# More buffers, a re-ordered convolution loop and a lighter final stage in a kernel that trains a gated FFN beside an S4 convolution

## The chip, the cores and the metric

One core of one Trainium2 chip. The metric is device time in microseconds (us) of one execution; lower is better. The kernel before took 1850.78 us (median of 6, 1848.61 to 1853.17).

## The reference, cut to what matters

A layer norm feeds two branches, a state-space convolution with a skip and a gated FFN; the sum with the input is the output. The kernel computes the output and all gradients for an incoming gradient of the same shape.

```python
def _A_ref(u, ...):                          # L, D, N = 2048, 576, 128
    K = einsum("dn,dnl,dn->dl", C, exp(dt*A*l), dt*B).real
    y = irfft(rfft(u, 2L) * rfft(K, 2L))[:L]
    return y + u * Dskip
def _B_ref(x, W_gate, W_up, W_down):         # F = 4608
    return (relu(x @ W_gate) * (x @ W_up)) @ W_down
x = A_u
xn = layernorm(x)
out = x + _A_ref(xn, ...) + _B_ref(xn, ...)
# ... cut: jax.vjp of this function; 13 outputs
```

## The kernel before

Everything runs on one core. The FFN goes over 12 chunks of F and keeps TensorE busy. The S4 branch is a generator that is advanced beside it: the Fourier transforms are matmuls, the spectra are multiplied on VectorE. Every generator yields an estimate of its own length, and the S4 branch is advanced as long as its sum stays below 0.9 of the FFN's. The last convolution stage is `p3` of the second half; after it the last FFN chunk also carries the final stage, in which the convolution's result, the FFN and the layer norm's gradient are added up. When the program is built, a scheduler then fixes the order of each engine's instructions.

Names of tiles (buffers) that come up often: osx is an output tile of the FFN, fA a result of the first transform, s_ug and s_k are spectra of the signals and of the convolution's kernel, pr_t, pr_w and pr_z belong to their product, fC is a result of the last transform ("unmix"; "mix" makes the spectra). hN, dgT, duT, hT and upm are the FFN's. To evict is to copy a result out of PSUM, where matmuls leave it.

```python
PACE = 0.9
# ... cut
        self.op = pool("ffn_o", 3)                       # osx: two output tiles' halves
# ... cut: an output tile of the FFN, stored with accumulation
            nc.gpsimd.dma_start(g.acc_dram[:, t, :, :], o[:], accum_op=ALU.add)
# ... cut: product of two spectra, conj for the gradient
        t = wpool.tile([P, 2, DH], BF16, name="pr_t")
        w = wpool.tile([P, 2, DH], BF16, name="pr_w")
        v.tensor_tensor(t[:], A, B, op=ALU.mult)
        v.tensor_tensor(w[:, 0, :], A[:, 0, :], B[:, 1, :], op=ALU.mult)
        v.tensor_tensor(w[:, 1, :], A[:, 1, :], B[:, 0, :], op=ALU.mult)
        Z = pool.tile([P, 2, DH], BF16, name="pr_z")
        # two sums on 64 partitions from t into Z[0:64], two from w into Z[64:P]
# ... cut: last stage of the convolution, h = 0..16
                old, Z = Z, None
                if h < ST:
                    # ... mix the kernel's spectrum into sk
                    Z = self.product(zp, pp, sg[:, 0], sk[:], False), self.product(zp, pp, sg[:, 1], sk[:], True)
                    yield 0.7
                if old is not None:
                    for i in range(2):
                        Ct = fp.tile([P, 2, 1, DH], BF16, name="fC2")
                        yield from self.unmix(Ct[:, :, 0, :], old[i])
                        nc.sync.dma_start(self.mix_in(self.C[2][hf], h - 1)[:, :, i:i + 1, :], Ct[:])
                        yield 0.5
# ... cut: final stage; load() runs two row tiles ahead
        nc.vector.tensor_tensor(base[:], xg[:], self.dsk[:].unsqueeze(1).to_broadcast([P, 2, D]), op=ALU.mult)
# ... cut: take() of each half of each output
        self.g.nc.vector.tensor_tensor(dst, base[:, i, cols], ps, op=ALU.add)
```

## Time and profile before

| | before |
|---|---|
| median, us | 1850.78 |
| profiled execution: span, us | 1848.1 |
| TensorE busy, us | 1740.9 |
| half-clock stretches of TensorE, us | 34 in seven pieces |

Two more views are needed later. First the last three parts of the run as windows (start and end, length, then busy us of TensorE, its weight loads, VectorE, ScalarE and GpSimd with their numbers of instructions, TensorE's clock, DMA share and GB/s). They are the last convolution stage, the rest of the chunk, and the last chunk with the final stage:

```profile
1536.00:1616.00 80.00, 68.13 (x446) 37.23 (x444) 73.95 (x247) 58.22 (x159) 6.91 (x8) 0.96 0.89 241
1616.00:1698.00 82.00, 79.16 (x658) 54.65 (x656) 19.67 (x42) 26.90 (x61) 6.90 (x8) 0.98 0.67 185
1698.00:1808.00 110.00, 98.14 (x765) 68.81 (x763) 90.91 (x200) 47.83 (x93) 0.00 (x0) 1.00 0.69 217
```

VectorE has three different lives: over nine tenths busy, a quarter busy, and over eight tenths busy. TensorE is short of work, or of released work, in the first and the third: 11.9 of 80 and 11.9 of 110 us idle.

Second, one product on VectorE (start, length, engine, line, operation, tiles, count):

```profile
1607.62 0.46 DVE L665 TENSOR_TENSOR pr_t<-s_ug,s_k 128x576 bf16<-128x576 bf16 x1
1608.00 0.30 DVE L666 TENSOR_TENSOR pr_w<-s_ug,s_k 128x288 bf16<-128x288 bf16 x1
1608.22 0.30 DVE L667 TENSOR_TENSOR pr_w<-s_ug,s_k 128x288 bf16<-128x288 bf16 x1
1608.43 0.61 DVE L671 TENSOR_TENSOR pr_z<-pr_t 64x288 bf16<-64x288 bf16 x2
1609.08 0.64 DVE L674 TENSOR_TENSOR pr_z<-pr_w 64x288 bf16<-64x288 bf16 x2
```

The records of the multiplications overlap: the next starts 0.22 us after one that lasts 0.30.

### The profile page before, as it was taken

What the parts mean: (1) busy time and instruction counts of PE and PEld (TensorE: products, weight loads), DVE (VectorE), ACT (ScalarE), POOL (GpSimd) and SP (SyncE); (2) the same over time, 40 slices, a digit from 0 to 9 for tenths busy, and PEclk for the clock granted to TensorE, in tenths of its full rate; (3) what the DMA queues carried; (4) which work ended last, traced back from release to release, by engine and by line L of the source; (5) the groups of instructions that cost most, each with busy time, mean ns of one, the idle gap of its engine ahead of it and who ended that gap; (6) DMA issues with size and microseconds to landing.
All of it is one profiled execution on the core that took longest, in us unless ns stands there. A gap on an engine that the chain in (4) does not pass through costs nothing. (4 is left out here: it accounts for less than half of the span.)

```text
span 1848.1 us, 41883 instructions
## 1 busy us (share of the span) xinstructions
PE 1740.9 (94%) x16257; PEld 1180.4 (64%) x16257; DVE 1378.3 (75%) x3223; ACT 1173.1 (63%) x2647; POOL 205.9 (11%) x246
## 2 busy tenths in 40 slices
PE   7989989999999999999999999998999998899988
PEld 5655547667666666766666766766666765476666
DVE  7565975786897787787887889889878757923882
ACT  5865855686587488477477567657747737732442
POOL 0200002111012012002102101202201100010000
PEclk9989989999999999999999999999999999999999
DMA  8798989668567566766676756855755779885763
GB/s 292 264 325 290 338 235 269 194 174 237 168 129 205 185 178 169 210 187 149 189 202 136 234 157 153 235 163 121 188 166 115 163 240 268 220 213 159 247 214 100
DMA packets 236411, 373.26 MB, mean 202 GB/s; under 512 B 49202, under 2 KB 153140, under 8 KB 234676
## 3 DMA queue, kind: packets, MB, share of 16 engines
q1 hardware_dynamic: 210244, 304.08, 50.6%
q0 software_dynamic: 24384, 51.92, 18.1%
q10 hardware_dynamic: 1584, 14.60, 2.3%
q8 instruction: 127, 2.08, 0.5%
q14 instruction: 72, 0.59, 0.1%
HBM read 233.08 MB, written 137.43 MB: 200 GB/s over the span
## 5 line engine op out<-in xcount | busy, mean ns | idle before, releaser
L244 PE MATMUL ps_mm<-xT,wd 128*128 128x512 bf16 x1440 | 357.0, 379 | 0.7 <-ACT xT L153 0.7
L244 PEld LDWEIGHTS <-wd 128*128 128x128 bf16 x2145 | 194.9, 98 | 179.6 <-issue 8.5
L68 ACT CAST osx<-ps_mm 128x288 bf16<-128x288 f32 x684 | 261.9, 423 | 72.9 <-PE ps_mm L300 59.8
L313 POOL DMA_DIRECT2D acc_dram<-osx x160 | 139.3, 875 | 1037.8 <-ACT osx L68 581.5
L300 PE MATMUL ps_mm<-wf,dgT 128*128 128x288 bf16 x1152 | 209.0, 288 | 18.0 <-ACT osx L68 12.8
L354 PEld LDWEIGHTS <-rows 128*128 128x128 bf16 x1536 | 145.9, 98 | 98.2 <-issue 4.2
L300 PE MATMUL ps_mm<-wf,duT 128*128 128x288 bf16 x1152 | 207.6, 288 | 0.0
L300 PE MATMUL ps_mm<-wf,hT 128*128 128x288 bf16 x1152 | 185.4, 287 | 8.0 <-ACT osx L68 2.4
L929 DVE TENSOR_TENSOR pr<-X,ps_s 128x256 f32<-128x256 f32 x288 | 120.4, 418 | 85.1 <-PE ps_s L925 82.7
L244 PE MATMUL ps_mm<-gT,wd 128*128 128x512 bf16 x705 | 178.6, 379 | 0.4 <-ACT obw L68 0.4
L254 DVE SCALAR_TENSOR_TENSOR upm<-rg,ps_mm 128x512 bf16<-128x512 bf16 x144 | 98.4, 684 | 99.8 <-PE ps_mm L244 82.9
L68 ACT COPY YT<-ps_s 128x1024 bf16<-128x1024 bf16 x144 | 146.9, 1020 | 22.7 <-PE ps_s L911 20.1
L338 PE MATMUL ps_mm<-rows,hN 128*128 128x144 bf16 x2304 | 159.9, 229 | 0.0
L338 PEld LDWEIGHTS <-hN 128*128 128x128 bf16 x2304 | 150.7, 99 | 7.8 <-issue 5.2
L300 PEld LDWEIGHTS <-dgT 128*128 128x128 bf16 x1152 | 109.5, 98 | 55.3 <-issue 27.5
L354 PE MATMUL ps_mm<-duN,rows 128*128 128x384 bf16 x768 | 138.6, 326 | 0.5 <-DVE upm L254 0.5
L354 PE MATMUL ps_mm<-dgN,rows 128*128 128x384 bf16 x768 | 136.6, 326 | 1.3 <-DMA rows<-xs_dram 1.3
L300 PEld LDWEIGHTS <-hT 128*128 128x128 bf16 x1152 | 107.1, 98 | 41.3 <-issue 12.0
L300 PEld LDWEIGHTS <-duT 128*128 128x128 bf16 x1152 | 113.0, 98 | 29.8 <-issue 0.2
L68 ACT CAST obw<-ps_mm 128x384 bf16<-128x384 f32 x105 | 50.0, 477 | 127.0 <-PE ps_mm L354 90.8
L68 ACT CAST dhb<-ps_mm 128x512 bf16<-128x512 f32 x141 | 83.8, 595 | 63.7 <-PE ps_mm L244 62.1
L930 DVE TENSOR_REDUCE Sm<-pr 128x8 f32<-128x256 f32 x288 | 120.0, 417 | 3.6
(215 smaller groups left out, 3148.5 us busy)
## 6 DMA issues: line engine op xcount, KB each, us to landing
acc_dram<-osx POOLq DMA_DIRECT2D x176, 288.0 KB, 4.6
gT<-in_gT_dram SPq DMA_DIRECT2D x48, 640.0 KB, 6.4
xT<-xT_dram SPq DMA_DIRECT2D x44, 640.0 KB, 5.8
rows<-in_gq_dram SPq DMA_DIRECT2D x48, 576.0 KB, 4.4
rows<-xs_dram SPq DMA_DIRECT2D x48, 512.0 KB, 5.3
wd<-in_Wd_dram SPq DMA_DIRECT2D x36, 480.0 KB, 5.6
wf<-in_Wf_dram ACTq DMA_DIRECT2D x11, 1296.0 KB, 9.1
ex_dram<-exs SPq DMA_DIRECT2D x18, 640.0 KB, 5.3
```

The source lines that it names most:

```text
L68: self.nc.scalar.copy(out, in_)
L244: nc.tensor.matmul(ps[:], lhsT=w[:, k, fs], rhs=rhs[:, k, :], start=(k == 0), stop=(k == NK - 1))
L254: nc.vector.scalar_tensor_tensor(upm[:], rg[:], 0.0, ps_u[:], op0=ALU.is_gt, op1=ALU.mult)
L300: nc.tensor.matmul(ps[:, :DH], lhsT=lt, rhs=rh, start=(i == 0), stop=(i == len(mms) - 1))
L313: nc.gpsimd.dma_start(g.acc_dram[:, t, :, :], o[:], accum_op=ALU.add)
L338: nc.tensor.matmul(ps[:, ft * 144:(ft + 1) * 144], lhsT=self.hN[:, st, ft * P:(ft + 1) * P], rhs=gq[:, st, :], start=(st == 0), stop=(st = ...
L354: nc.tensor.matmul(ps[:, :Fc], lhsT=xs[:, st, 0:P], rhs=src[:, st, :], start=(st == 0), stop=(st == ST - 1))
L929: nc.vector.tensor_tensor(pr[:], X[:, dx:dx + DG, r0:r0 + 2].rearrange("p d r a -> p d (r a)").unsqueeze(2).to_broadcast(sh), psg[:, 0:DG ...
L930: nc.vector.tensor_reduce(out=Sm[:, vi, s0 + dd:s0 + dd + DG, :], in_=pr[:], op=ALU.add, axis=AX.X)
```

## The change

Its intent is to take the waits away that TensorE's list shows: a fourth osx buffer; the exponentials of the first stage in halves with 8 buffers and a pool of their own for the first transform's outputs (fA); deeper pools and an interleaved order in the last convolution stage; a product with one scratch buffer, which pays for these buffers; and a final stage in which ScalarE evicts and sums rows, while the skip becomes part of the convolution kernel's first tap.

```diff
-        self.op = pool("ffn_o", 3)
+        self.op = pool("ffn_o", 4)
 ... (exponentials: par_ex 3 -> 8 buffers, tiles of SX instead of 2*SX, twice as many steps)
-            yield from self.fwd1(hf, 2, load, ap, n, gap)
+            yield from self.fwd1(hf, 2, load, ap, self.pool(c, f"p1_o{hf}", 2 * n - 2 * (n < 4), "right"), n, gap)
 ... (the same in p3; p1_f, p3_f: 2 -> n buffers, p3_z: 3 -> n; n is 4 in the first and the last stage, else 2)
         v.tensor_tensor(t[:], A, B, op=ALU.mult)
-        v.tensor_tensor(w[:, 0, :], A[:, 0, :], B[:, 1, :], op=ALU.mult)
-        v.tensor_tensor(w[:, 1, :], A[:, 1, :], B[:, 0, :], op=ALU.mult)
 ... (the two sums from t)
+        v.tensor_tensor(t[:, 0, :], A[:, 0, :], B[:, 1, :], op=ALU.mult)
+        v.tensor_tensor(t[:, 1, :], A[:, 1, :], B[:, 0, :], op=ALU.mult)
 ... (the two other sums, now from t)
                     yield from self.mix(sk[:], b[:, :, 0, :])
-                    Z = self.product(zp, pp, sg[:, 0], sk[:], False), self.product(zp, pp, sg[:, 1], sk[:], True)
-                    yield 0.7
-                if old is not None:
-                    for i in range(2):
-                        ... (unmix of old[i], store)
-                        yield 0.5
+                    yield 0.35
+                for i in range(2):
+                    if h > 0:
+                        ... (unmix of Z[i], store)
+                    if h < ST:
+                        Z[i] = self.product(zp, pp, sg[:, i], sk[:], i == 1)
+                    yield 0.7
 ... (skip: Kst[0:1, 0, :] += dsk, once per group of 32 channels)
-        nc.vector.tensor_tensor(base[:], xg[:], self.dsk[:].unsqueeze(1).to_broadcast([P, 2, D]), op=ALU.mult)
-        self.g.nc.vector.tensor_tensor(dst, base[:, i, cols], ps, op=ALU.add)
+        if i == 0:
+            self.g.bal.copy(self.o[:, 0, cols], ps, DH)
+        else:
+            self.g.nc.scalar.activation(self.dx[:, cols], ps, ACT.Copy, accum_out=self.m[:, hf:hf + 1])
```

More of the change, by code (lines that the diff above doesn't have):

```diff
@@ L294, in outdx @@
                     mms = [(Ts[ft][1], self.wf[:, 1, ft, hs]) for ft in range(FTC)] + [(Ts[ft][2], self.wf[:, 2, ft, hs]) for ft in range(FTC)]
-                mms = [(lt[:, js], rh) for lt, rh in mms]
+                mms = [(lt[:, js], rh, slice(0, DH)) for lt, rh in mms]
                 if last is not None:
-                    mms = last.terms(t, which, hf) + mms
+                    mms = [(a, b, slice(0, DH)) for a, b in last.terms(t, which, hf)] + mms
                 ps = g.psum_mm.tile([P, 512], F32, name="ps_mm")
-                for i, (lt, rh) in enumerate(mms):
-                    nc.tensor.matmul(ps[:, :DH], lhsT=lt, rhs=rh, start=(i == 0), stop=(i == len(mms) - 1))
+                for i, (lt, rh, cs) in enumerate(mms):
+                    nc.tensor.matmul(ps[:, cs], lhsT=lt, rhs=rh, start=(i == 0), stop=(i == len(mms) - 1))
                 if last is None:
@@ L303, in outdx @@
                 else:
-                    last.take(t, which, hs, ps[:, :DH])
+                    last.take(t, which, hf, hs, ps[:, :DH])
                 next(src, None)
@@ L566, in params @@
             pool = self.pool(c, "par_raw", 1)
-            exp_ = self.pool(c, "par_ex", 3)
+            exp_ = self.pool(c, "par_ex", 8)
             raw = pool.tile([P, 6, D], BF16, name="raw")
@@ L581, in ex_step @@
             def ex_step(i):
-                shp = [P, 2 * SX, NE]
+                shp = [P, SX, NE]
                 ex = exp_.tile(shp, F32, name="exs")
-                v.tensor_tensor(ex[:], pw[:, 0, i * SX:(i + 2) * SX].unsqueeze(2).to_broadcast(shp), self.ev[:].unsqueeze(1).to_broadcast(shp), op=ALU.mult)
+                v.tensor_tensor(ex[:], pw[:, 0, i * SX:(i + 1) * SX].unsqueeze(2).to_broadcast(shp), self.ev[:].unsqueeze(1).to_broadcast(shp), op=ALU.mult)
                 nc.scalar.activation(ex[:], ex[:], ACT.Exp)
-                nc.sync.dma_start(self.ex_dram[:, i:i + 2], ex[:].rearrange("p (i d) e -> p i d e", d=SX))
-                bal.add(d=1.4, a=1.2)
-            for i in range(0, 8, 2):
+                nc.sync.dma_start(self.ex_dram[:, i], ex[:])
+                bal.add(d=0.75, a=0.65)
+            for i in range(0, 8):
                 ex_step(i)
-                yield 2.0
+                yield 1.0
             p1 = pool.tile([P, D], F32, name="p1")
@@ L601, in params @@
                 yield 2.0
-            for i in range(8, D // SX, 2):
+            for i in range(8, D // SX):
                 ex_step(i)
-                yield 2.0
+                yield 1.0
     def dft(self, pool, dram):
@@ L612, in dft, with fwd1 @@
         return load
-    def fwd1(self, hf, ns, load, ap, n, gap):
+    def fwd1(self, hf, ns, load, ap, op, n, gap):
         g, nc = self.g, self.g.nc
@@ L622, in fwd1 @@
                     yield gap
-            A = ap.tile([P, 2, ns, DH], BF16, name=f"fA{ns}")
+            A = op.tile([P, 2, ns, DH], BF16, name=f"fA{ns}")
             for ri in range(2):
@@ L662, in product @@
         t = wpool.tile([P, 2, DH], BF16, name="pr_t")
-        w = wpool.tile([P, 2, DH], BF16, name="pr_w")
+        Z = pool.tile([P, 2, DH], BF16, name="pr_z")
         v = nc.vector
         v.tensor_tensor(t[:], A, B, op=ALU.mult)
-        v.tensor_tensor(w[:, 0, :], A[:, 0, :], B[:, 1, :], op=ALU.mult)
-        v.tensor_tensor(w[:, 1, :], A[:, 1, :], B[:, 0, :], op=ALU.mult)
-        Z = pool.tile([P, 2, DH], BF16, name="pr_z")
         for i in range(2):
@@ L671, in product @@
             v.tensor_tensor(Z[0:64, i, :], t[r, 0, :], t[r, 1, :], op=ALU.add if conj else ALU.subtract)
+        v.tensor_tensor(t[:, 0, :], A[:, 0, :], B[:, 1, :], op=ALU.mult)
+        v.tensor_tensor(t[:, 1, :], A[:, 1, :], B[:, 0, :], op=ALU.mult)
         for i in range(2):
             r = slice(i * 64, (i + 1) * 64)
-            v.tensor_tensor(Z[64:P, i, :], w[r, 1, :], w[r, 0, :], op=ALU.subtract if conj else ALU.add)
+            v.tensor_tensor(Z[64:P, i, :], t[r, 1, :], t[r, 0, :], op=ALU.subtract if conj else ALU.add)
         g.bal.add(d=1.6)
@@ L698, in load @@
                 return lambda i, n2: t[:, i, n2 % 2, :]
-            yield from self.fwd1(hf, 2, load, ap, n, gap)
+            yield from self.fwd1(hf, 2, load, ap, self.pool(c, f"p1_o{hf}", 2 * n - 2 * (n < 4), "right"), n, gap)
         with ExitStack() as c:
             bp = self.pool(c, f"p1_b{hf}", n, "right")
-            fp = self.pool(c, f"p1_f{hf}", 2, "right")
+            fp = self.pool(c, f"p1_f{hf}", n, "right")
             pp = self.pool(c, f"p1_p{hf}", 1, "right")
@@ L764, in load @@
                 return lambda i, n2: kk[:, :, n2 % 4, :]
-            yield from self.fwd1(hf, 1, load, ap, n, gap)
+            yield from self.fwd1(hf, 1, load, ap, self.pool(c, f"p3_o{hf}", 2 * n - 2 * (n < 4), "right"), n, gap)
         with ExitStack() as c:
             bp = self.pool(c, f"p3_b{hf}", n, "right")
-            fp = self.pool(c, f"p3_f{hf}", 2, "right")
-            zp = self.pool(c, f"p3_z{hf}", 3, "right")
+            fp = self.pool(c, f"p3_f{hf}", n, "right")
+            zp = self.pool(c, f"p3_z{hf}", n, "right")
             pp = self.pool(c, f"p3_p{hf}", 1, "right")
@@ L778, in p3 @@
             bs = Ahead(load_b, ST, n)
-            Z = None
+            Z = [None, None]
             for h in range(ST + 1):
-                old, Z = Z, None
                 if h < ST:
@@ L787, in p3 @@
                     yield from self.mix(sk[:], b[:, :, 0, :])
-                    Z = self.product(zp, pp, sg[:, 0], sk[:], False), self.product(zp, pp, sg[:, 1], sk[:], True)
-                    yield 0.7
-                if old is not None:
-                    for i in range(2):
-                        Ct = fp.tile([P, 2, 1, DH], BF16, name="fC2")
-                        yield from self.unmix(Ct[:, :, 0, :], old[i])
-                        nc.sync.dma_start(self.mix_in(self.C[2][hf], h - 1)[:, :, i:i + 1, :], Ct[:])
-                        yield 0.5
+                    yield 0.35
+                for i in range(2):
+                    if h > 0:
+                        Ct = fp.tile([P, 2, 1, DH], BF16, name="fC2")
+                        yield from self.unmix(Ct[:, :, 0, :], Z[i])
+                        nc.sync.dma_start(self.mix_in(self.C[2][hf], h - 1)[:, :, i:i + 1, :], Ct[:])
+                    if h < ST:
+                        Z[i] = self.product(zp, pp, sg[:, i], sk[:], i == 1)
+                    yield 0.7
     def p2_pools(self, c):
@@ L809, in p2 @@
         lv, parp, dkp, exp_, xp, xop, uvp, yop, ytp, gp = pools
+        self.kdp = parp
         pend, turned = [], []
@@ L903, in turn @@
         if dd + DG == SC:
+            h0 = hf * DH + gi * SC
+            dsk = self.kdp.tile([1, SC], BF16, name="dsk")
+            nc.sync.dma_start(dsk[:], self.Dskip[h0:h0 + SC].rearrange("(o d) -> o d", o=1))
+            nc.vector.tensor_tensor(Kst[0:1, 0, :], Kst[0:1, 0, :], dsk[:], op=ALU.add)
             nc.sync.dma_start(self.k_dram[hf][:, :, gi], Kst[:].rearrange("p (q a) d -> p q a d", q=4))
@@ L1040, in load @@
             pool = lambda name, bufs: self.ctx.enter_context(g.tc.tile_pool(name=name, bufs=bufs, reuse_waits="tile"))
-            self.dsk = pool("fin1", 1).tile([P, D], BF16, name="dsk")
-            nc.sync.dma_start(self.dsk[:], self.Dskip.rearrange("(o d) -> o d", o=1).to_broadcast([P, D]))
+            one = pool("fin1", 1)
+            self.nr = one.tile([P, ST], F32, name="nr")
+            nc.vector.tensor_scalar(self.nr[:], g.rinv[:], -1.0 / D, None, op0=ALU.mult)
             self.pool = pool("fin3", 3)
@@ L1055, in load @@
         nc.sync.dma_start(acc[:], g.acc_dram[:, t])
-        base = self.pool.tile([P, 2, D], F32, name="f_base")
-        nc.vector.tensor_tensor(base[:], xg[:], self.dsk[:].unsqueeze(1).to_broadcast([P, 2, D]), op=ALU.mult)
-        g.bal.add(d=1.2)
-        return S3, Ct, xt, xg, acc, base
+        return S3, Ct, xt, xg, acc
     def begin(self, t):
@@ L1065, in begin, with skip @@
         self.o = self.pool.tile([P, 2, D], BF16, name="f_o")
+        self.dx = self.pool.tile([P, D], F32, name="f_dx")
+        self.m = self.pool.tile([P, 5], F32, name="f_m")
+    def skip(self, hf):
+        h0 = hf * DH
+        for k in range(NK):
+            c0, c1 = max(k * P, h0), min((k + 1) * P, h0 + DH)
+            if c0 < c1:
+                yield k, slice(c0 - k * P, c1 - k * P), slice(c0 - h0, c1 - h0)
     def terms(self, t, i, hf):
-        S3, Ct, xt, xg, acc, base = self.parts[t]
+        S3, Ct, xt, xg, acc = self.parts[t]
         cols = slice(hf * DH, (hf + 1) * DH)
@@ L1071, in terms, with take @@
         return mms + [(self.g.ident_bf[:], r) for r in ([xt[:, cols]] if i == 0 else []) + [acc[:, i, cols]]]
-    def take(self, t, i, cols, ps):
-        base = self.parts[t][5]
-        dst = self.o[:, 0, cols] if i == 0 else base[:, 1, cols]
-        self.g.nc.vector.tensor_tensor(dst, base[:, i, cols], ps, op=ALU.add)
-        self.g.bal.add(d=0.37)
+    def take(self, t, i, hf, cols, ps):
+        if i == 0:
+            self.g.bal.copy(self.o[:, 0, cols], ps, DH)
+        else:
+            self.g.nc.scalar.activation(self.dx[:, cols], ps, ACT.Copy, accum_out=self.m[:, hf:hf + 1])
+            self.g.bal.add(a=0.4)
     def end(self, t):
         g, nc = self.g, self.g.nc
-        S3, Ct, xt, xg, acc, base = self.parts[t]
-        o = self.o
-        inv_d = 1.0 / D
-        xn, gt, dx = xg[:, 0, :], xg[:, 1, :], base[:, 1, :]
+        S3, Ct, xt, xg, acc = self.parts[t]
+        o, m, dx = self.o, self.m, self.dx[:]
+        xn, gt = xg[:, 0, :], xg[:, 1, :]
         nc.sync.dma_start(g.out0_v[:, t, :], o[:, 0, :])
-        m = self.pool.tile([P, 4], F32, name="f_m")
-        nc.scalar.activation(acc[:, 1, :], dx, ACT.Copy, accum_out=m[:, 0:1])
-        nc.vector.scalar_tensor_tensor(acc[:, 0, :], dx, 1.0, xn, op0=ALU.mult, op1=ALU.mult, accum_out=m[:, 1:2])
-        nc.vector.tensor_scalar(m[:, 2:3], m[:, 1:2], -inv_d, None, op0=ALU.mult)
-        nc.vector.tensor_scalar(m[:, 3:4], m[:, 0:1], -inv_d, g.rinv[:, t:t + 1], op0=ALU.mult, op1=ALU.mult)
-        nc.vector.scalar_tensor_tensor(dx, xn, m[:, 2:3], dx, op0=ALU.mult, op1=ALU.add)
-        nc.scalar.activation(dx, dx, ACT.Identity, scale=g.rinv[:, t:t + 1], bias=m[:, 3:4])
+        nc.vector.scalar_tensor_tensor(acc[:, 0, :], dx, 1.0, xn, op0=ALU.mult, op1=ALU.mult, accum_out=m[:, 2:3])
+        nc.vector.tensor_scalar(m[:, 3:4], m[:, 2:3], -1.0 / D, None, op0=ALU.mult)
+        nc.vector.tensor_scalar(m[:, 4:5], m[:, 0:1], m[:, 1:2], self.nr[:, t:t + 1], op0=ALU.add, op1=ALU.mult)
+        nc.vector.scalar_tensor_tensor(dx, xn, m[:, 3:4], dx, op0=ALU.mult, op1=ALU.add)
+        nc.scalar.activation(dx, dx, ACT.Identity, scale=g.rinv[:, t:t + 1], bias=m[:, 4:5])
         nc.vector.tensor_tensor(o[:, 1, :], dx, gt, op=ALU.add)
         nc.sync.dma_start(g.out1_v[:, t, :], o[:, 1, :])
-        g.bal.add(d=2.5, a=1.1)
+        g.bal.add(d=2.2, a=0.6)
 @with_exitstack
@@ L1195, in lay_out @@
     o["gq"] = gr.reshape(P, ST, 4, 144).transpose(2, 0, 1, 3)
+    dsk = zeros(NK, P, P)
+    for d, v in enumerate(inputs["A_Dskip"]):
+        dsk[d // P, d % P, d % P] = v
+    o["dsk"] = dsk.transpose(1, 0, 2)
     g, u, dn = inputs["B_W_gate"], inputs["B_W_up"], inputs["B_W_down"]
```

## The prediction

> **What bounds the kernel now.** I read the page first: engine shares, then the slices.
>
> ```profile
> span 1848.1 us, 41883 instructions
> ...
> PE 1740.9 (94%) x16257; PEld 1180.4 (64%) x16257; DVE 1378.3 (75%) x3223; ACT 1173.1 (63%) x2647; POOL 205.9 (11%) x246
> ...
> PE   7989989999999999999999999998999998899988
> ...
> PEclk9989989999999999999999999999999999999999
> DMA  8798989668567566766676756855755779885763
> ```
>
> TensorE bounds the whole run: it is idle for 1848.1 - 1740.9 = 107 us. The change gives it no work and takes none: both instruction orders hold the same matmuls, in another order. So every gain must come out of these 107 us, or out of time in which the clock is low. The slices show where that is: the first seventh, and the last quarter of the span. The middle is at 9 throughout.
>
> Next, TensorE's own list of waits, longest first:
>
> ```profile
> PE ps_mm L300 <- ACT osx L68: 15.2, 24, 2.2
> ...
> PE ps_s L654 <- ACT fC L68: 8.5, 8, 1.7
> PE pt L273 <- DVE dgT L262: 7.9, 7, 2.8
> PE ps_s L627 <- ACT fA L68: 7.7, 9, 3.2
> PE ps_s L684 <- DMA bC<-C_dk: 5.6, 1, 5.6
> PE ps_mm L300 <- DVE f_o L1076: 3.8, 4, 1.2
> ```
>
> Columns: total us, times, longest. The names are those of tiles whose pools the change deepens (osx, fC, fA) and of the final stage it rewrites (f_o; most of dgT, below). Only bC is not touched. That is some 43 us of the 107; many others are gaps too short to be listed.
>
> Third, windows around the longest stalls, for the granted clock (PEclk), and one window of the last convolution stage:
>
> ```profile
> 135.20:142.00 6.80, 5.84 (x45) 5.37 (x45) 2.64 (x4) 4.43 (x8) 0.00 (x0) 0.50 0.95 320
> 1647.30:1650.70 3.40, 3.40 (x32) 3.40 (x30) 0.00 (x0) 0.03 (x1) 0.86 (x1) 0.50 0.84 280
> ...
> 1590.00:1600.00 10.00, 8.22 (x57) 4.32 (x56) 9.57 (x33) 7.50 (x21) 0.86 (x1) 1.00 0.82 201
> ```
>
> Columns after the length: busy PE, PEld, DVE, ACT, POOL, clock, DMA share, GB/s. A stall of about 3 us is followed by 3.4 or 6.8 us at half clock. There are seven such stretches (at 108, 135, 244, 268, 1555, 1582 and 1647 us), 34 us together, which cost up to 17 us. In the last row VectorE is the full engine, 9.57 of 10 us, not TensorE.
>
> Last, the timeline at two stalls:
>
> ```profile
> 1645.49 0.82 DVE L62 CAST osx<-ps_mm 128x288 bf16<-128x288 f32 x2 [4.04 <-DMA acc_dram<-osx]
> 1646.00 0.53 PE L300 MATMUL ps_mm<-wf,dgT 128*128 128x288 bf16 x3 [2.84 <-DVE osx L62]
> ```
>
> An eviction has no free osx buffer until the accumulating store has landed; TensorE waits behind it.
>
> ```profile
> 1759.19 1.36 DVE L1057 TENSOR_TENSOR f_base<-f_xg,dsk 128x1152 f32<-128x1152 bf16 x1 [2.31 <-DMA f_xg<-in_grad_out_dram]
> 1760.47 0.42 DVE L262 TENSOR_TENSOR dgT<-dhb,upm 128x512 bf16<-128x512 bf16 x1
> ...
> 1760.95 0.40 PE L273 MATMUL pt<-ident_bf,dgT 128*128 128x128 bf16 x4 [2.81 <-DVE dgT L262]
> ```
>
> In the final stage the skip product stands at the head of VectorE's queue, waits for a load that nobody needs yet, and holds the FFN's dgT behind it.
>
> **What the Trainium skill says.** "TensorE: Matmul & The Clock Gate", Part 1 (the HAM clock gate): after an idle window of about 3.4 us the array runs at half clock until it has been busy for one. The windows above agree (0.50 for 3.4 or 6.8 us after stalls of 2.8 to 5.6 us), so a removed stall of 3 us should give back 1.7 to 3 us more. The same page, Part 1, on queue depths: ScalarE and VectorE are strictly first in, first out; the dgT line above is that. "Perfetto Trace Analysis", Identifying Performance Opportunities: a recurring gap on the engine that should be full can mean too few buffers; the osx waits agree. "DMA: Bandwidth & Descriptors", Issuing engines are not separate DMA queues: all transfers share 16 engines. In the first part the DMA share is 0.77 to 1.02, so deeper pools there hide latency but add no bandwidth.
>
> **The change, part by part** (us of TensorE's time).
>
> (1) osx pool from 3 to 4. A group of four output tiles is made at about 2.2 us each (18 matmuls of 0.122 us), and a store takes 4.6 us to land in the median (7.4 at 1638 us) plus 0.9 us of issue on GpSimd. Three tiles cover about 4.4 us, four 6.6. ScalarE waits 10.4 us and VectorE 4.0 us on that store over the run. TensorE's osx waits are 15.2 + 2.8 = 18 us; the part that is not a buffer but a busy ScalarE stays. I take 11 us, plus two or three half-clock stretches of 3.4 us (about 4 us): **-15**, of which 4 at 1646 us, 4 at 243, the rest in the middle.
>
> (2) fA in its own pool of 8 for the first half, and the exponentials in halves with 8 buffers. The stall at 136 us (3.2, ScalarE waiting for an A_ug store) and its 6.8 us at half clock go: -6. The stall at 106 us (2.9) does not: there three exponential inputs of 1.43 us stood ahead of an fA eviction on VectorE; the new order puts six halves of about 0.82 there, no shorter. Deeper s_ug: -1. The DMA is full here (0.95 to 1.02), so I count **-5**, not -7.
>
> (3) The last convolution stage. It holds 32 products; their VectorE rows sum to 19.4 + 19.2 + 14.6 + 9.7 + 9.7 = 72.6 us, with 11 us of FFN work, in 81 us. So VectorE is the bound there, and the 11.6 us that ScalarE waits for fC stores is mostly beside it. The product keeps all its operations (the second buffer goes, the number of instructions does not), so the stage stays VectorE-bound. What changes is the order: between its first mix and its last unmix stood 144 + 91 + 80 FFN matmuls (41.7 us at 0.122, 0.216 and 0.056), now 213 + 120 + 108 (58.0 us), while FFN work on VectorE grows from 11 to 15.6. With 11.7 us of its own matmuls: before 80 us of time for 53 of TensorE work; after about 90 for 70. **-8**, and one half-clock stretch, -1.5. The fA and b_k waits just before: -1.5. Sum **-11**.
>
> (4) The final stage. VectorE loses the product (16 x 1.357 = 21.7 us), and 64 additions from PSUM (16 x 4 x 0.45 = 28.7); ScalarE takes 64 evictions instead (0.42 each; half of them with an accumulator read of 0.19), and loses the sum pass (16 x (0.683 + 0.186) = 13.9). Per row tile VectorE falls from about 5.9 to 2.7 us, ScalarE rises from 1.7 to 2.9, against 3.9 us of TensorE work: ScalarE fits. The listed stalls from 1694 us on: f_o 3.8, f_base 1.2, dgT 6.2 of its 7.9; with short gaps about 12.8. I leave 2: **-11**.
>
> (5) The skip as a term of the kernel's first tap: 18 small additions and 18 loads of 64 bytes. In the new order each load is issued right after the previous addition, some 60 us before use; no wait. 18 x about 0.15 us on VectorE: **0**.
>
> Sum: -15 - 5 - 11 - 11 = -42. Stalls do not vanish alone: the scheduler has moved hundreds of instructions, and time gained ahead of a transfer is partly waited at the next. The bC wait (5.6) may grow when TensorE comes earlier. I charge +7: **-35, 1816 us**.
>
> **The rivals.** (a) The convolution's VectorE bound dominates: fC buffers and reordering give nothing. For it: 9.57 of 10 us busy. Against: VectorE was busy for only 1.9 of 10 us right after (1620 to 1630), so spreading helps. Time: about 1826. (b) The start is DMA-bound, so that stalls move from fA and osx to loads (bC, b_ug, rows). For: share around 1. Against: ends by 330 us. Gain only 25: about 1826. (c) ScalarE becomes the bound at the end: its evictions queue behind the scaling pass that waits for VectorE. For: that pass waited 14.6 us from 1695 us on. Against: three PSUM banks cover 2 to 3 us, and the new order puts two evictions ahead of it. Would give back 5 to 8 us: about 1823. (d) Everything listed goes, with the clock at full: 43 + 17 - 6 = 54 us, about 1796.
>
> **Range and chances.** The threshold of 2% is at 1814, beside my estimate. Between rivals (a) to (c) singly and most of (d) I put 1800 to 1832 at 8 in 10. Faster by over 2%: 0.42; within: 0.57; slower: 0.01, since nothing is added to TensorE.
>
> **What would show it.** PE busy near 1741 - 8 (half-clock stretches gone) with idle about 80. osx waits on TensorE below 8, with no "DMA acc_dram<-osx" wait on ScalarE above 2 us; fA stall at 136 gone, 106 kept; at most three or four half-clock stretches; in the last convolution stage VectorE above 9 of 10 over a longer stretch; in the final stage no wait of VectorE for f_xg and TensorE idle under 3 us. Wrong if osx waits stay (then a busy ScalarE was the cause), if a new wait on f_dx appears above 5 us, or if the first 330 us take as long as before.

## The result, and the profile after

The changed kernel took 1806.97 us (median of 8, 1803.12 to 1809.65) against 1851.09 for the kernel before beside it. The ratio is 0.9758 (0.9747 to 0.9769): 2.4% faster. Ratios here are the mean time of one kernel's runs over that of the other's of the same rounds, so not quite the ratio of the medians quoted; in brackets stands the 95% interval. Gains in us below are (1 - ratio) x 1852, about the median of the kernel before; for the whole change that is 44.8 us.

The page of the changed kernel, and TensorE's longest waits (us in total, times, longest):

```profile
span 1805.7 us, 41964 instructions
...
PE 1731.2 (96%) x16257; PEld 1174.3 (65%) x16257; DVE 1354.6 (75%) x3193; ACT 1189.7 (66%) x2716; POOL 205.5 (11%) x246
...
PE   7989989999999999999999999998999999999999
...
PEclk9999999999999999999999999999999999999999
```

```profile
PE ps_mm L211 <- DMA gT<-in_gT_dram: 7.4, 1, 7.4
PE ps_mm L300 <- ACT osx L68: 5.9, 13, 1.5
PE ps_s L654 <- DVE pr_z L673: 5.2, 16, 0.6
PE ps_mm L300 <- DVE hT L256: 4.2, 4, 2.4
PE ps_s L683 <- DMA bC<-C_dk: 4.0, 2, 3.3
```

Idle time of TensorE fell from 107 to 74.5 us, and its half-clock stretches from 34 to 17 us, four pieces instead of seven. The 42.4 us between the two profiled spans are 32.7 of idle time and 9.7 of busy time, for the same matmuls: 17 us less at half clock is up to 8.5 us of it. The osx wait went from 15.2 to 5.9 us. The first line is the kernel's first load, which nothing in the change touches. Two small ones grew: VectorE's pr_z, which releases the last stage's unmixing (1.5 us before), and hT (2.0 before).

The windows of the last three parts, to be held against those of the kernel before:

```profile
1521.00:1611.00 90.00, 83.48 (x574) 44.91 (x574) 82.98 (x259) 71.65 (x186) 10.36 (x12) 1.00 0.86 238
1611.00:1670.00 59.00, 59.00 (x519) 40.74 (x517) 13.45 (x30) 14.97 (x33) 3.45 (x4) 1.00 0.69 221
1670.00:1766.00 96.00, 96.00 (x761) 68.86 (x760) 57.14 (x135) 59.77 (x149) 0.00 (x0) 1.00 0.80 250
```

The convolution stage is 10 us longer, yet holds 574 matmuls instead of 446; the rest of the chunk is 23 us shorter. The final stage has no idle TensorE at all: 96.00 of 96 us busy. How much earlier TensorE reached the same matmul (a landmark) tells where the gain came from: 11.2 us by 285 us, 4.2 between there and the last matmul that reads the convolution's kernel (1513 us, just before the last stage), 13 more by the first matmul of the final stage (1670 us), 14 in the final stage.

### The profile page after: what moved, and what is told of

Its sections match the earlier page's.

```text
span 1805.7 us, 41964 instructions
## 1 busy us (share of the span) xinstructions
PE 1731.2 (96%) x16257; PEld 1174.3 (65%) x16257; DVE 1354.6 (75%) x3193; ACT 1189.7 (66%) x2716; POOL 205.5 (11%) x246
```

## The experiments

All results below were correct. Each run stands beside the kernel before on the same chip; the runs were made on three chips, so runs are compared by their ratios, and their medians only give a second figure. "The ledger" is the prediction's list of parts (1) to (5).

### The parts alone

The exponentials, the fA pool of the first stage and its s_ug pool, alone:

```diff
+            exp_ = self.pool(c, "par_ex", 8)            # and halves: SX instead of 2 * SX
+            yield from self.fwd1(hf, 2, load, ap, self.pool(c, f"p1_o{hf}", ...), n, gap)
+            fp = self.pool(c, f"p1_f{hf}", n, "right")
```

> Only the start of the change: exponentials in halves with 8 buffers, the first transform's outputs (fA of the first stage) in a pool of their own, deeper s_ug pool. Theory A (the ledger: each part is worth its own stalls): -5 us, 1846; the stall at 136 us and its half-clock stretch shorter, the one at 106 us kept, and the gain of about 5 us already there at the first landmark after 330 us and carried unchanged to the end. Rival B (reading by place: TensorE reached the 296-us landmark 11 us earlier in the changed kernel, so the start is worth more than its listed stalls): -11 us, 1840. Rival C (the start is DMA-bound; time gained is paid back at the loads of chunk 1): 0 to -2 us.

Measured: 1843.82 us, ratio 0.9951 (0.9933 to 0.9969), so 9.1 us. That is nearer to the reading by place than to the ledger. But not for the ledger's reason: the stall at 136 us is still there (3.3 us, at 138). The pieces of this part are tried in the last experiment.

The convolution's part alone:

```diff
+            yield from self.fwd1(hf, 1, load, ap, self.pool(c, f"p3_o{hf}", ...), n, gap)
+            # product with one scratch buffer; p3_f and p3_z n deep; interleaved loop, as in the change
```

> Only the convolution's part: own fA pool in the last stage's first transform, product with one scratch buffer, deeper fC and Z pools, mix, product and unmix interleaved. Theory A (VectorE bounds this stage, and the new order spreads the same VectorE work over more FFN matmuls): -11 us, 1840, nearly all of it between the last kernel load and the end of the stage; VectorE busy there still above 9 of 10. Rival B (by place, with the osx wait at 1646 us in it): -13. Rival C (VectorE's total is unchanged, so the work spread later collides with the final stage, whose VectorE work is still heavy here): -3 us or less, with the gain at the end of the stage lost again in the final stage.

Measured: 1848.7 us, ratio 0.9981 (0.9970 to 0.9992), so 3.5 us. Rival C holds. TensorE reached the first matmul of the final stage 6.2 us earlier than in the kernel before and ended only 2.2 us earlier. The timeline of this kernel in the final stage shows where it went:

```profile
1754.40 1.36 DVE L1056 TENSOR_TENSOR f_base<-f_xg,dsk 128x1152 f32<-128x1152 bf16 x1 [3.77 <-DMA f_xg<-in_grad_out_dram]
1755.68 0.42 DVE L262 TENSOR_TENSOR dgT<-dhb,upm 128x512 bf16<-128x512 bf16 x1
...
1756.15 0.40 PE L273 MATMUL pt<-ident_bf,dgT 128*128 128x128 bf16 x4 [4.02 <-DVE dgT L262]
```

It is the stall that the prediction shows of the kernel before at 1759 us. There VectorE waited 2.31 us for the load and TensorE 2.81; here 3.77 and 4.02.

The final stage alone, with the skip in the first tap:

```diff
-        nc.vector.tensor_tensor(base[:], xg[:], ...)     # and the additions from PSUM
+        # begin, take, end, skip in Kst: as in the change
```

> Only the final stage: evictions and row sums on ScalarE, no skip product, skip added to the kernel's first tap. Theory A: -11 us, 1840, all of it after the first matmul of the final stage (1698 us before). Rival B (by place): -14. Rival C (without deeper fC and osx buffers the final stage starts as late, and ScalarE becomes the bound): -5. The first tap's 18 small additions cost nothing: landmarks up to 1335 us within 1 us of the kernel before.

Measured: 1836.06 us, ratio 0.9911 (0.9892 to 0.9929), so 16.5 us. In the profile, whose span is 15.3 us shorter, 13.7 us come between the first matmul of the final stage and the last chunk's weight gradients. TensorE's list of waits after 1690 us is empty in this run, as in the changed kernel. The skip's 18 additions cost nothing that shows; the landmarks up to 1335 us wander by up to about 3 us (briefly 4), more than the 1 us expected, and are back at 0.3 by 1477.

The fourth osx buffer alone does not fit: the next pool needs 2.25 kB per partition and 1.375 are left. It was run with the one-buffer product and one Z buffer less in the other half:

```diff
+        self.op = pool("ffn_o", 4)
+        # product with one scratch buffer
-            zp = self.pool(c, f"p3_z{hf}", 3, "right")
+            zp = self.pool(c, f"p3_z{hf}", 3 if hf else 2, "right")
```

> Only the fourth osx buffer; to make room for it, the product uses one scratch buffer, and one Z buffer of the other half's convolution stage goes (its own control runs next). Theory A (the ledger): -15 us, 1836: 4 us at 243, 4 at 1646, the rest in the middle, no wait of ScalarE for the accumulating store above 2 us, osx waits on TensorE below 8. Rival B (the waits were for a busy ScalarE, not for a buffer): -2 to -5 us, the osx waits on TensorE stay near 15.

Measured: 1845.98 us, ratio 0.9965 (0.9952 to 0.9977), so 6.5 us, between the two theories. The wait of ScalarE for the accumulating store is gone, yet the stall at 243 us stays with its 2.2 us:

```profile
243.47 0.40 ACT L68 CAST s_ug<-ps_s 128x288 bf16<-128x288 f32 x1 [2.81 <-DMA S_ug<-s_ug]
...
244.22 0.66 PE L300 MATMUL ps_mm<-wf,hT 128*128 128x288 bf16 x3 [2.23 <-ACT osx L68]
```

So there it was a late ScalarE, not a missing osx buffer: ScalarE had stood for 2.81 us on an eviction that waited for an s_ug buffer still being stored. By place, this run gained nothing up to 1528 us, then 8 us by the start of the final stage, and lost 4.6 of these in it. The 8 us cannot be put down to the osx buffer, because the one-buffer product changes the last convolution stage too (below). The control for this run was not made: the undo below asks the same question more directly.

The four sum to 35.6 us, the whole change gave 44.8. It is not a clean sum: the one-buffer product is in two of the four.

### Do the parts help each other?

Convolution and final stage together:

```diff
+        # both parts as above, nothing else
```

> The convolution's part and the final stage together, nothing else. Alone they gave -3.5 and -16.5 us. Theory A (TensorE reached the final stage 6 us earlier in the convolution kernel but lost 4 of them there, because VectorE's skip product waited for loads that did not come earlier; without that product the 4 us stay): -24, 1829. Rival B (the parts add up): -20, 1833. Rival C (they overlap): -17, 1836.

Measured: 1830.63 us, ratio 0.9868 (0.9846 to 0.9891), so 24.5 us, as theory A said; the sum of the two is 20. The interval, 20 to 28.5, leaves simple addition at its edge, but overlap (17) is out, and the place speaks for A: from the first matmul of the final stage to the last chunk's weight gradients this run needs 95.6 us, the convolution kernel 113.5, the kernel before 109.4. The convolution part is worth 3.5 us before the final stage is mended and about 8 after.

The changed kernel with three osx buffers:

```diff
-        self.op = pool("ffn_o", 4)
+        self.op = pool("ffn_o", 3)
```

> The changed kernel with the osx pool back at 3. Theory A (the fourth buffer was worth 6.5 us alone, with 4.6 us more lost to the skip product in the final stage, which is gone here): 11 us slower than the changed kernel, 1818; the wait of ScalarE for the accumulating store is back at about 10 us. Rival B (the ledger's -15): 1822. Rival C (6.5, as alone): 1813.5.

Measured: 1815.7 us, ratio 0.9784 (0.9761 to 0.9808). Against the changed kernel that is 4.8 us by the ratios and 8.7 by the medians; the two were not run in the same rounds, and the intervals just overlap (all six times, 1812.1 to 1818.4, lie above the changed kernel's). So the buffer is worth 5 to 9 us, less than theory A's 11 and well under the ledger's 15. In the profile the wait of ScalarE for the store is back (12.1 us, one of 5.2 at 1626 us), and TensorE's osx wait is 13.9 us.

### What in the convolution part does the work?

A product that runs without interruption takes 2.09 us in the kernel before (median of 54) and 2.35 in the changed one (of 28). The changed kernel's:

```profile
1600.01 0.45 DVE L665 TENSOR_TENSOR pr_t<-s_ug,s_k 128x576 bf16<-128x576 bf16 x1
1600.49 0.62 DVE L668 TENSOR_TENSOR pr_z<-pr_t 64x288 bf16<-64x288 bf16 x2
1601.14 0.31 DVE L669 TENSOR_TENSOR pr_t<-s_ug,s_k 128x288 bf16<-128x288 bf16 x1
1601.37 0.30 DVE L670 TENSOR_TENSOR pr_t<-s_ug,s_k 128x288 bf16<-128x288 bf16 x1
1601.70 0.64 DVE L673 TENSOR_TENSOR pr_z<-pr_t 64x288 bf16<-64x288 bf16 x2
```

The operations are the same and last as long, but now a sum follows the multiplication that it reads, twice. It starts after that one has ended: 0.49 us after a start where the next multiplication used to follow after 0.375, and 0.336 where it used to be 0.219. That is 0.12 us twice, nearly the whole 0.25. (The expectation below blames the multiplications that wait for the sums; their steps are about as long as before, 0.338 us against 0.334.) So two scratch buffers ought to be better:

```diff
+        w = wpool.tile([P, 2, DH], BF16, name="pr_w")    # the old product in the convolution's part
```

> The convolution's part as in the first call, but the product keeps its two scratch buffers. In the traces a product that runs without interruption takes 2.09 us with two scratch buffers and 2.35 us with one, because two multiplications must now wait for the sums that read the buffer. Theory A (this dependency ate the part's gain: 32 products x 0.25 us = 8 us of VectorE in the stage that VectorE bounds, 96 x 0.25 = 24 us over the run): 5 to 8 us better than with one buffer, so 1841 to 1844, VectorE busy about 11 us less over the run. Rival B (the gain was lost in the final stage, not in the product): within 2 us of the 1848.7 of the one-buffer form.

Measured: 1855.89 us, ratio 1.0009 (0.9995 to 1.0023). Not 5 to 8 us better than with one buffer but 5 worse: both theories fell. The same in the changed kernel, where there is room for the second buffer (the first and the last stage):

```diff
+        w = t
+        if two:                                          # two = (n == 4)
+            w = wpool.tile([P, 2, DH], BF16, name="pr_w")
+            # both multiplications into w here
```

> The changed kernel, but with the product's two scratch buffers in the two stages that run alone (the first of the first half, the last of the second), where there is room for them. Theory A (dependency in the product, VectorE-bound stage): 16 + 32 products x 0.25 us = 4 + 8 us less of VectorE there, of which TensorE sees 4 to 8: 1799 to 1803, and the time from the last kernel load to the end of the stage is shorter. Rival B (the new order already hides it behind FFN work): within 2 us of 1807.

Measured: 1815.09 us, ratio 0.9784 (0.9760 to 0.9809): 5 to 8 us slower than the changed kernel, so both theories fell again. (Here too the intervals just overlap; the times, 1814.0 to 1815.4 against 1803.1 to 1809.7, do not.) The windows of the last stage explain it, from the first mix to the last unmix; the convolution kernel with two buffers, then the same with one, then this one (the changed kernel's window is shown above):

```profile
1540.00:1617.00 77.00, 65.39 (x445) 34.09 (x445) 73.03 (x246) 59.36 (x158) 6.90 (x8) 1.00 0.88 238
```

```profile
1536.00:1626.00 90.00, 82.47 (x564) 44.62 (x570) 82.94 (x259) 71.52 (x186) 10.35 (x12) 1.00 0.84 222
```

```profile
1525.00:1602.30 77.30, 65.79 (x449) 34.33 (x449) 73.78 (x248) 60.25 (x161) 6.90 (x8) 1.00 0.90 249
```

With two buffers the stage is over sooner, as it should, but holds only 449 matmuls, and TensorE idles for 11.5 us instead of 6.5. Of the FFN's matmuls, the traces show 315 between the stage's first mix and its last unmix in the kernel before, 318 in both two-buffer kernels, and 441 in the changed kernel and its undo with three osx buffers; the convolution kernel with one buffer has 433 (some of its records are missing). The osx run has 441 with the old loop. So it was not the interleaved loop that put FFN work into the stage, it was the single scratch buffer: with it, the order of instructions comes out with more FFN matmuls between the stage's own. Why the scheduler orders them so, no trace can show.

New theory D: the buffer gains only by that order, and costs its 0.25 us. Then the old product with a slower pace of this stage, which buys the same order openly, must be at least as good:

```diff
+        # two scratch buffers in the last stage only (p3, n == 4)
-                    yield 0.35
+                    yield 0.35 * (1.5 if hf else 1.0)
-                    yield 0.7
+                    yield 0.7 * (1.5 if hf else 1.0)
```

> The changed kernel with the product's two scratch buffers in the last convolution stage only, and that stage's own pace slowed by 1.5, so that about as much FFN work of TensorE stands between its first mix and its last unmix (56 us by program order) as in the changed kernel (58); the two-buffer form without the slower pace had 42. Theory D (what matters is how much FFN work the stage is spread over; the single scratch buffer gained only because it made the emission order spread out): equal to the changed kernel or up to 3 us faster, 1804 to 1807, the last unmix at about the same place as in the changed kernel. Rival E (the single buffer gains in itself, by leaving gaps between VectorE's product steps in which the FFN's work gets through): 3 to 4 us slower than the changed kernel, 1811.

Measured: 1799.15 us, ratio 0.9709 (0.9687 to 0.9731): 53.9 us, 8 to 9 better than the changed kernel. Rival E fell, and theory D had the direction but not the size (up to 3 us). 429 FFN matmuls are in the stage, which now needs 81.3 us for them and not 89.7; 32 products that are 0.25 us shorter are 8 of these 8.4 us. Of the 10.4 us that the profile gained by the final stage, 6.6 come from the stage and the rest of its chunk. The other 3.8 were there before it, where the order of TensorE's instructions is the same in both kernels: this execution happened to have fewer half-clock stretches (6.8 us in all, the changed kernel's 17), which is not the edit's doing. Not run was the slower pace with one scratch buffer, which would part the two edits.

And further, with 2.0 in place of 1.5:

```diff
-                    yield 0.35 * (1.5 if hf else 1.0)
+                    yield 0.35 * (2.0 if hf else 1.0)    # and 0.7 likewise
```

> The same with the pace slowed by 2.0: 72 us of FFN work inside the stage, where TensorE then has about as much to do (72 + 16 of its own) as VectorE (73 + about 20). Theory D: TensorE's idle time in the stage (6.5 us of 90 in the changed kernel) falls to about 2: 1801 to 1804, faster than both kernels. Rival E: as the run above, 1811. Rival F (the stage now ends so late that the final stage waits for its stores or loads): slower than the run above by 2 or more.

Measured: 1795.42 us, ratio 0.9687 (0.9667 to 0.9708): 58 us, the fastest of all kernels here and again more than theory D gave it. Its stage, and that of the 1.5 kernel for comparison:

```profile
1519.60:1611.80 92.20, 90.58 (x734) 59.59 (x734) 83.16 (x268) 72.84 (x197) 13.80 (x16) 1.00 0.98 272
```

```profile
1517.50:1598.80 81.30, 75.42 (x558) 45.17 (x558) 77.23 (x256) 66.73 (x181) 10.35 (x12) 1.00 0.93 252
```

TensorE's idle time in the stage goes 11.9 (before), 6.5 (changed), 5.9 (1.5), 1.6 (2.0). Here 12.0 us are gained on the changed kernel between the last matmul that reads the convolution's kernel and the final stage. Rival F did not come: the final stage again has no listed wait. The two paced kernels' intervals overlap, so the step from 1.5 to 2.0 rests on the stage's own numbers.

### What in the final stage does the work?

The kernel before, with the skip product moved from two tiles ahead to its own tile:

```diff
-        nc.vector.tensor_tensor(base[:], xg[:], ...)     # in load(n), n up to t + 2
+        self.g.nc.vector.tensor_tensor(base[:], xg[:], ...)   # in begin(t)
```

> The kernel before, with one thing moved: the skip product of a row tile is computed when the tile's turn comes and not two tiles earlier, right after its loads are issued. VectorE's work is the same to the instruction. Theory A (it is the queue: a product at the head of VectorE's queue waits for a load that nobody needs yet): the dgT stalls of the final stage go (6.2 us) and with them what follows from them: -6 to -10 of the -16.5 us of the final stage's part. Rival B (it is the amount: VectorE was 91 of 110 us busy there, and only taking its work away helps): -2 or less.

Measured: 1849.54 us, ratio 0.9977 (0.9968 to 0.9986), so 4.3 us: between the theories. TensorE's waits after 1690 us, before and with the product moved:

```profile
PE pt L273 <- DVE dgT L262: 6.2, 3, 2.8
...
PE ps_mm L300 <- DVE f_base L1076: 1.2, 2, 0.8
```

```profile
PE ps_mm L300 <- DVE f_o L1077: 4.4, 6, 1.2
PE ps_mm L300 <- DVE f_base L1077: 3.1, 3, 1.8
PE ps_mm L300 <- DVE upm L254: 1.0, 1, 1.0
PE pt L273 <- DVE dgT L262: 0.9, 1, 0.9
```

The dgT wait went as theory A said, 6.2 to 0.9 us, but other waits for VectorE took back 3.5 of it: f_o and f_base together went from 5.0 (3.8 of f_o, in the prediction's list) to 7.5, and upm is new with 1.0. VectorE still waited 9.9 us for f_xg (12.1 before). So the queue is at most about a quarter of the 16.5 us (by place, this run's profile gains only 1.3 us in the final stage, 108.1 against 109.4). The rest came with the work taken off VectorE, which was busy for 90.91 of 110 us and is so for 57.14 of 96 in the changed kernel.

### What in the start does the work?

Only the pools of the first stage, exponentials whole:

```diff
+            yield from self.fwd1(hf, 2, load, ap, self.pool(c, f"p1_o{hf}", ...), n, gap)
+            fp = self.pool(c, f"p1_f{hf}", n, "right")
```

> The kernel before with only the pools of the first stage changed: a pool of 8 for the first transform's outputs (2 and 2 in the second half) and deeper s_ug; the exponentials stay whole. With the exponentials in halves as well it gave -9 us. The ledger's claim: -5, the stall at 136 us gone with its half-clock. Rival B (the halves of the exponentials were the larger part, because an eviction now waits for 0.8 us of VectorE and not for 1.4): -3 or less, and the stall at 136 us stays.

Measured: 1847.63 us, ratio 0.9972 (0.9962 to 0.9983), so 5.2 us: the ledger's size, but not its place. By the landmarks it gains nothing up to 200 us and 3.6 us between 200 and 250: there the stall at 243 us and its half clock are gone, because ScalarE no longer waits for an s_ug buffer. By the place and the wait it was the s_ug pool, which the ledger gave 1 us, and not the fA pool. The halves of the exponentials bring the other 3.9 of 9.1 (the intervals of the two runs overlap); with them TensorE was 3.9 us ahead by 150 us. The pools' run at 136 us:

```profile
136.10 1.49 DVE L584 TENSOR_TENSOR exs<-pw,ev 128x1280 f32<-128x1280 f32 x1 [6.40 <-DMA ex_dram<-exs]
137.51 1.28 DVE L62 CAST fA<-ps_s 128x288 bf16<-128x288 f32 x3
138.02 0.28 PE L627 MATMUL ps_s<-sig,Sx 128*128 128x288 bf16 x1 [4.31 <-DVE fA L62]
```

With ScalarE's wait for the A_ug store gone, the stall is longer: 4.31 us. VectorE stands for 6.40 us on an exponential that waits for a store of an earlier one, with three evictions behind it. That wait was in the kernel before too, at the same moment:

```profile
135.07 1.49 DVE L584 TENSOR_TENSOR exs<-pw,ev 128x1280 f32<-128x1280 f32 x1 [5.55 <-DMA ex_dram<-exs]
135.71 0.70 ACT L68 CAST fA<-ps_s 128x288 bf16<-128x288 f32 x2 [3.25 <-DMA A_ug<-fA]
136.16 0.40 PE L627 MATMUL ps_s<-sig,Sx 128*128 128x288 bf16 x1 [3.24 <-ACT fA L68]
```

Two engines were stuck, and TensorE's list named the one that came last. In the changed kernel 2.0 us of this stall are left, and VectorE is still the releaser.

## Why the prediction was right, and where not

The time was right: 1807 lies in 1800 to 1832, 9 us below the 1816. The bound, the method (only idle time of TensorE and half clock can be gained) and the totals held: idle 74.5 against "about 80", busy 1731.2 against 1733, four half-clock stretches against three or four. But the terms were less right than their sum: (1) was too large, (2) and (4) too small, and that they nearly cancel is luck. The chances leaned a little to the wrong side: the text gave "faster by over 2%" 0.42 and "within" 0.57, and it was faster by 2.4%. The rule behind the half-clock terms, that a stall of about 3 us is followed by half clock, does not hold in the kernel before's own trace (see the last section).

- **(1) osx, -15.** Mis-sized: 5 to 9 by the undo. The stall of the last chunk is the buffer's (3.9 us and 6.8 us at half clock come back at 1626 us with three buffers). The 4 us at 243 us are not: four buffers leave that stall as it was, and the deeper s_ug pool of part (2) takes it away without a fourth osx buffer. The step that failed is the wait: TensorE waited for ScalarE, and ScalarE for another pool. By the landmarks, 4.0 us are lost up to the last stage without the buffer, against 11 in the ledger for the start and the middle.
- **(2) the start, -5.** Mis-sized and wrongly reasoned: 9.1. "The stall at 136 us goes" is wrong, since VectorE's own wait lay under the named one (2.0 us of it are left); the stall at 106 us, which the ledger kept at 2.9, split into 1.8 and 1.4. The gain comes from the pools (5.2, of which 3.6 are at 243 us, where the ledger credits osx) and from the halves (3.9), which the ledger gave nothing. By 285 us the changed kernel is 11.2 us ahead and the start's part alone 5.4 by the same landmark; the further 6 us are not explained by any run here (the osx buffer is not it: with three the kernel is 12.8 us ahead there).
- **(3) the last convolution stage, -11.** The bound and the mechanism were right: VectorE is the full engine, and what counts is the FFN work that it is spread over; the counts, 315 and 441, were right too. The step that failed is "The product keeps all its operations [...] What changes is the order": it took the one-buffer product to be free, and did not see that the order comes from it. The single scratch buffer, not the new loop, made that order, and it also makes each product 0.25 us longer, 8 us over 32 products in the stage. Alone the part gave 3.5 us, with the final stage mended about 8. The old product with a slower pace gets the order without the price, and gains 8 to 12 us more by the medians.
- **(4) the final stage, -11.** Mis-sized: 16.5 alone (13 to 20; 13.7 in the stage by the profile). The ledger counted 12.8 us of stalls and left 2; in the changed kernel none is left (11.9 us idle before, 0 after), and TensorE's busy time for the stage fell from 98.14 to 96.00 us besides. The time before the stage counts too: what the convolution part gained was waited away here while the skip product stood in the queue.
- **(5) the skip, 0.** Held.
- **The +7 for new waits** failed. The reasoning was that time gained ahead of a transfer is waited at the next. That does happen (4 of 6.2 us in the convolution kernel), but the change removes that very wait, so parts gain more together than one by one: 24.5 for the convolution and the final stage, against 20. The bC wait fell from 5.6 to 4.0 us instead of growing.

Of the rivals, (a) was half true: VectorE's bound did stay, but spreading helped, and further spreading helped more. (b) is out: the DMA share stays near 1 in the start, yet TensorE gained 11.2 us there and the bC wait did not grow. (c) did not come: TensorE has no listed wait in the final stage, though VectorE waits for ScalarE's f_dx evictions there, 22.6 us in all. The prediction named such a wait above 5 us as a sign of being wrong; it came and cost nothing, since TensorE was busy for 96.00 of 96 us. (d), 54 us, was missed by this change and reached, by another way, by the paced kernel.

## What to carry to other kernels

When a stage is bound by a side engine, ask first how much of the main engine's work the program order puts inside it: here that one number, set by a pacing constant, was worth more than the stage's buffers. A buffer saved can change the schedule more than the waits, so a gain must be undone piece by piece before it is credited. And a wait in the list names only the last of the things that were missing; look at what stands at the head of every queue involved before counting it as gone.

## What the Trainium skill lacked or had wrong

- "VectorE: DVE Perf Modes", The DRAIN you can't avoid, measures for eight copies that a semaphore after each costs nothing extra. Here a wait for the operation just before did cost: the same sum starts 0.336 us after the multiplication that it reads and 0.219 us after one that it does not read; with a like step after the first multiplication, that is 2.35 against 2.09 us per product. The same section does say that an operation which isn't held starts earlier, and the overlapping records agree.
- "TensorE: Matmul & The Clock Gate", Part 1, gives an idle window of about 3.4 us as what brings half clock. Here shorter stalls do it, and their length does not decide: stalls of 2.0 us (at 135 us of the changed kernel), 2.2 (243, before) and 2.4 (572, changed) were each followed by 3.4 us at half clock, while one of 2.3 at 1117 (changed) and three of 2.8 to 2.9 us (1266, 1761 and 1793, before) were not. What tells them apart in the changed kernel is where they fall. Its half-clock stretches begin whole steps of 3.413 us apart (at 104.7, 135.5, 261.7 and 572.4 us: 9, 37 and 91 steps), like the page's free-running window; in the 3.413 us before each, TensorE was busy for 44, 41, 12 and 39%, and the emptiest such slot that no stretch follows was busy for 46% (1115 us). So what counts there is how much of one such slot a stall fills. In the kernel before, the two groups overlap (33 to 67% against 41% and more), so these traces give no sharp limit; the page gives none.
- "Perfetto Trace Analysis", Identifying Performance Opportunities, gives too few buffers as a cause of repeated gaps. With a fourth buffer one of the osx gaps stayed at 2.23 us. The page says to find what blocks the engine with the gap; it lacks the next step, what blocks the engine waited for: here ScalarE had waited 2.81 us for a store out of another pool, s_ug.
- No page has a measure for the pacing of a side stage ("Perfetto Trace Analysis", Optimization Strategy, only says that interleaving regimes with different bottlenecks may help). Here, with the same instructions in the stage, 318, 429 and 602 FFN matmuls inside it left TensorE idle for 11.5, 5.9 and 1.6 us of it.
